# More Strassen pairs in groups 2 to 5, with the side work around them moved: a fused attention and SwiGLU kernel on one core

## The chip, the cores and the metric

The kernel runs on one core of a Trainium2 chip. The metric is the device time of one execution in microseconds; a kernel's time is the median of its timed runs. Below, PE is TensorE, DVE is VectorE, ACT is ScalarE, POOL is GpSimd and SP is SyncE. Each engine gets its instructions in one fixed order; the engines meet through semaphores.

The profile's own span (from first to last instruction) is some 1.8 us shorter than the device time of the same run.

Busy times hide short gaps. A matmul of 256 columns is recorded as 273 ns long, but in a full stream the next one starts after 109 ns; so a gap of up to some 0.16 us doesn't show in PE's busy time, and a wait in the list of waits is shown that much too short. Where it matters below, gaps are taken from the starts.

## The reference, cut to what matters

```python
def phi(x):
    return np.where(x > 0, x, np.exp(x) - 1.0) + 1.0
q_p, k_p = phi(q), phi(k)                          # q, k, v: (8, 8, 576, 64)
kv  = np.einsum('bhsd,bhse->bhde', k_p, v)
z   = np.sum(k_p, axis=2)
num = np.einsum('bhsd,bhde->bhse', q_p, kv)
den = np.einsum('bhsd,bhd->bhs', q_p, z)[..., None] + 1e-06
x   = (num / den) ...                              # reshaped to (4608, 512)
g   = x @ w_gate                                   # (512, 1536)
val = x @ w_val
out = (g * sigmoid(g) * val) @ w_out               # (1536, 512)
```

## The kernel before

The 4608 tokens are handled in nine groups of 512 (g = 0 to 8). For each group the attention output x is made ready; **layer 1** multiplies it with `w_gate` and `w_val` in twelve blocks of 128 columns and forms hT = silu(gate) * val; **layer 2** multiplies hT with `w_out`. The work for later groups (exp and max of k and q, the key-value product "J", the x product "M") is woven in between. In groups 2 to 8 layer 2 is done by Strassen's scheme, seven products in place of eight, and in layer 1 `NP[g]` *pairs* of blocks are done so too. In such a pair the gate and value products of two blocks are formed together, as seven products of four 256-column matmuls where the plain way has the columns of eight; the sums of weights that it needs are called W1 sums below (`wl_sum`), those of x `x_sum`, those of h `h_sums`.

```python
    hT = two([P, FB, U * C], FP16, "hT")           # two buffers, by group parity
    NP = {2: 0, 3: 2, 4: 2, 5: 2, 6: 6, 7: 6, 8: 6}
    # a plain block is four chunks of two 512-column matmuls
    def c_chunk(g, fb, k, pg, pv):
        (src, dst) = ((wg, pg), (wv, pv))[k // 2]
        def mm():
            for i in (2 * (k % 2), 2 * (k % 2) + 1):
                nc.tensor.matmul(out=dst[:, :], lhsT=src[:, i, P * fb:P * fb + P], rhs=xT[i][g % 2][:, :],
                                 start=(i == 0), stop=(i == 3))
        op("PE", 0.432, mm, ...)
        if k == 1:
            op("ACT", 0.52, lambda: silu_1(pg[:, :], s[:, :]), ...)
        if k == 3:
            op("DVE", 0.6, lambda: c_mul(g, fb, pv, s), ...)
    # a pair of blocks by Strassen: product n of 7, four 256-column matmuls each
    def pair_prd(g, p, n, bx, bz, by, h22):
        ...
        op("PE", 0.437, lambda: prd_1(g, p, n, dst), r, [nm(dst)])
        # n = 1, 5, 6: a copy on ACT; n = 2: silu; n = 7: a sum on DVE; n = 3: a sum on DVE, silu
        # n = 4: two products on DVE that write hT
    def casts(b):
        for lp in range(2):
            op("ACT", 1.07, lambda lp=lp: vcast(b, lp), ["v16"], [f"vm{lp}"])
    # end of layer 2 of group g: the loads of batch g + 3 are queued together
            for (f, x) in ((ld_k, "k16"), (ld_q, "q16"), (ld_v, "v16")):
                op("LD", 0.75, lambda f=f: f(b3), [], [x])
    XE = {g: "AVAA" for g in range(NG)}            # the four x copies: ACT, DVE, ACT, ACT
    WL = {2: [(m, c, 0) for m in range(4) for c in range(2)], 3: [...3...], 4: [...3...], 5: [...2...]}
    ORDER = {g: "10 11 20 21 60 61 50 51 70 71 30 M 31 40 J 41" for g in (2, 3, 4)}
    ORDER[5] = "10 11 20 21 60 61 50 51 70 71 M 30 31 | 40 41 J"
    ...
    for i in steps.split():                        # one fixed order of all operations
        ops[int(i)][2]()
```

Each `op` records an engine, an estimated duration, an action, and what it reads and writes. Nothing is emitted in the order in which it is recorded: the string `steps` lists all of them by number in one fixed order, and that order is what each engine gets. In `ORDER`, "40" is product 4 of token half 0, and so on.

Of the kernel before, what the change touches and what calls it, by code (L numbers as in the profile page):

```python
# [13 lines left out]
P = 128  # L14
# [3 lines left out]
def kernel(  # L18
# [54 lines left out]
    hT = two([P, FB, U * C], FP16, "hT")  # L73
# [5 lines left out]
    wl2 = sb.tile([P, 2, 10 * P], FP16, name="wl2")  # L79
# [216 lines left out]
    def l1_gate(g, fb):  # L296
        (pg, pv), s = l1_banks(g, fb), sil[fb % 2]
        nc.scalar.activation(out=s[:, :], in_=pg[:, :], func=AF.Silu, bias=0.0, scale=1.0)  # L298
        nc.vector.scalar_tensor_tensor(out=hT[g % 2][:, fb, :], in0=pv[:, :], scalar=SC, in1=s[:, :],  # L299
                                       op0=ALU.mult, op1=ALU.mult)  # L300
# [12 lines left out]
    def thirds(t):  # L313
        f = t.rearrange("p a b -> p (a b)") if len(t.shape) == 3 else t.rearrange("p a b c -> p (a b c)")
        return [f[:, 6 * P * i:6 * P * i + 6 * P] for i in range(3)]

    wl_all = [sum((thirds(t) for t in ts), []) for ts in (
        (k16[0][:, :, :], q16[0][:, :, :], v16[0][:, :, :]), (kp[0][:, :, :], wl2[:, :, :], vm[0][:, :, :, :]))]
# [50 lines left out]
    def c_mul(g, fb, pv, s):  # L369
        nc.vector.scalar_tensor_tensor(out=hT[g % 2][:, fb, :], in0=pv[:, :], scalar=SC, in1=s[:, :],  # L370
                                       op0=ALU.mult, op1=ALU.mult)
# [4 lines left out]
    def l2(g, t, f0=0, f1=FB):  # L376
        pso[(g, t)] = (pV[0], pG[0], pV[1], pG[1])[t]
        for fb in range(f0, f1):
            nc.tensor.matmul(out=pso[(g, t)][:, :], lhsT=hT[g % 2][:, fb, P * t:P * t + P], rhs=wo[:, fb, :],  # L379
                             start=(fb == 0), stop=(fb == FB - 1))  # L380
# [16 lines left out]
    def h_blk(g, kh, th, f0, f1):  # L397
        return hT[g % 2][:, 2 * f0 + kh:2 * f1 - 1 + kh:2, HT * th:HT * th + HT]
# [24 lines left out]
    def prd(g, n, tt, fs, seeded):  # L423
# [5 lines left out]
        def left(f):  # L429
            h = hT[g % 2]  # L430
# [273 lines left out]
    def k_block():  # L704
        for lp in range(2):
            exp_(k16, ek, 1, lp)
            plus_1(k16, kp, 1, lp)
        for lp in range(2):
            least(ek[:, 2 * lp:2 * lp + 2, :], kp, 1, lp)

    def q_block():
        nc.scalar.preload_act_table_set("natural_log_exp_and_others")
        es = [eq1[:, 2 * J * D * (1 - lp):2 * J * D * (2 - lp)].rearrange("p (l x) -> p l x", l=2) for lp in range(2)]
        for lp in range(2):
            nc.scalar.activation(out=es[lp], in_=q16[1][:, 2 * lp:2 * lp + 2, :], func=AF.Exp, bias=0.0, scale=1.0)
            plus_1(q16, qp, 1, lp)
        z0_copy(1, 0)
# [7 lines left out]

    def first():
        sl = at(FB, [(7, k_block)])
        w = at(17, [
            (3, lambda: num8()), (3, lambda: z0(1, 0)), (3, lambda: z0(1, 1)), (3, q_block), (3, lambda: x8()), (7, lambda: t1(0)), (8, lambda: t1(1)),
# [122 lines left out]
    def rh(g, fbs, ths=(0, 1)):  # L852
        return [f"h{g % 2}.{fb}.{th}" for fb in fbs for th in ths]
# [4 lines left out]
    NP = {2: 0, 3: 2, 4: 2, 5: 2, 6: 6, 7: 6, 8: 6}  # L858
# [16 lines left out]
    def pair_prd(g, p, n, bx, bz, by, h22):  # L875
# [22 lines left out]
        if n == 4:  # L898
            fbs = [2 * p, 2 * p + 1]
            op("DVE", 0.6, lambda: mul_1(bx, ALU.mult, sl0, hT[g % 2][:, 2 * p:2 * p + 2, 0:HN]),  # L900
# [3 lines left out]
               lambda: eng.tensor_tensor(out=hT[g % 2][:, 2 * p:2 * p + 2, HN:2 * HN], in0=v22, in1=sl1, op=ALU.mult),  # L904
# [29 lines left out]
    def casts(b):  # L934
        for lp in range(2):
            op("ACT", 1.07, lambda lp=lp: vcast(b, lp), ["v16"], [f"vm{lp}"])

# [24 lines left out]
    def x_prd(g, lps=(0, 1)):  # L962
# [9 lines left out]
        if NP[g] and 1 in lps:  # L972
            rs = ([rx(g, 0), rx(g, 1)], [rx(g, 2), rx(g, 3), "xs0"], [rx(g, i) for i in range(4)], [rx(g, 2), rx(g, 3), "xs1"])
            for m in range(4):
                op("DVE", 0.35, lambda m=m: x_sum(g, m), rs[m], [f"xs{m}"])

    XE = {g: "AVAA" for g in range(NG)}

    def l2_prd(g, n, tt, fs=tuple(range(HF))):
# [7 lines left out]
        if HF - 1 not in fs:  # L987
            return
# [51 lines left out]
    PARTS = {"": tuple(range(HF)), "a": (0, 1, 2, 3), "b": (4, 5), "c": (4,), "d": (5,), "e": (0, 1, 2, 3, 4)}  # L1040

    def layer_1(g, fill, head):
# [28 lines left out]
        else:  # L1071
            slots = {7 * p + 2 * i: (p, k) for p in range(6) for (i, k) in enumerate(PSEQ[p == 5])}
            for s in range(48):
# [5 lines left out]
                elif s > 40 and head:  # L1079
# [10 lines left out]
    PSEQ = ((1, 5, 6, 2, 7, 3, 4), (1, 5, 6, 3, 7, 2, 4))  # L1090
    ZB = {g: 2 for g in range(NG)}
    LEAD = {g: 3 for g in range(NG)}
    H22 = {g: ["DVE"] * 6 for g in range(NG)}
    SPLIT_2 = {g: ((0, 6),) if NP.get(g) != 6 else ((0, 3), (3, 6)) for g in range(NG)}
    SPLIT = {g: ((0, 3), (3, 5), (5, 6)) if NP.get(g) == 6 else ((0, 4), (4, 6)) for g in range(NG)}
    WL = {2: [(m, c, 0) for m in range(4) for c in range(2)], 3: [(0, 0, 1), (0, 1, 1), (1, 0, 1)], 4: [(1, 1, 1), (2, 0, 1), (2, 1, 1)], 5: [(3, 0, 1), (3, 1, 1)]}

    def layer_2(g, done):
# [3 lines left out]
        if b3 < B:  # L1102
            for (f, x) in ((ld_k, "k16"), (ld_q, "q16"), (ld_v, "v16")):
# [10 lines left out]
    def step(g, x):  # L1114
# [5 lines left out]
        else:  # L1120
            l2_prd(g, int(x[0]), int(x[1]), PARTS[x[2:]])
# [7 lines left out]

    def program():  # L1130
        op("DVE", 1.05, lambda: phi_q(3, 1), ["q16", "eq1"], rqp(3, lps=[1]))
        for (f, x) in ((ld_k, "k16"), (ld_q, "q16"), (ld_v, "v16")):
            op("LD", 0.75, lambda f=f: f(4), [], [x])
        tail = []
        for g in range(2, NG):
# [8 lines left out]
        0 1 14 15 17 4 16 35 2 36 8 19 18 38 3 5 39 37 41 40 20 42 6 44 45 43 47 21 46 48 50 49 51 22 53 52 25  # L1144
        54 23 56 57 55 59 24 58 60 26 62 63 61 65 64 27 66 9 68 67 69 71 28 70 72 74 73 29 75 112 77 76 115 78
        10 13 80 79 81 83 7 82 84 104 12 86 85 87 89 105 88 90 11 92 91 93 95 118 94 96 30 98 121 99 97 101 31
        100 102 110 127 103 129 32 128 106 131 120 107 133 108 130 135 114 132 134 137 109 139 138 136 116 141
        140 122 143 142 111 33 145 147 144 117 34 124 113 150 159 148 151 125 146 149 162 153 160 126 152 154
        161 165 163 119 123 164 172 155 168 180 170 167 171 173 181 157 166 183 174 169 156 201 182 175 202 184
        158 204 176 203 206 205 185 208 207 186 209 211 350 210 213 187 212 215 214 216 349 218 217 220 219 223  # L1150
        224 221 227 225 229 222 231 191 230 232 192 228 234 233 236 235 238 237 193 239 179 226 241 194 243 245
        240 244 246 242 249 188 178 247 251 254 189 255 248 257 252 256 190 195 258 250 260 261 259 263 262 253
        264 289 266 278 267 265 269 268 270 279 272 271 273 286 275 274 282 276 284 301 277 303 280 302 305 292
        304 285 281 307 306 283 309 288 311 308 287 313 310 298 312 290 315 294 196 317 295 314 319 316 197 291
        321 320 324 318 297 322 299 333 326 300 336 334 328 293 339 337 325 296 327 346 341 342 340 345 354 343
        344 331 347 355 198 357 329 356 375 199 376 358 359 378 377 330 380 200 323 379 335 338 382 348 381 332
        383 360 385 384 177 387 386 361 389 388 390 392 460 391 394 397 393 398 395 401 403 362 402 399 405 404
        406 363 352 408 410 463 364 412 409 411 413 365 407 415 466 414 417 469 419 416 418 420 396 366 423 353
        425 424 428 429 400 431 421 430 432 426 434 422 435 433 437 427 436 438 370 440 452 441 439 443 442 444
        453 446 445 447 449 367 448 456 450 458 475 451 477 454 476 479 523 478 459 481 455 480 483 457 462 485  # L1160
        482 461 487 484 472 486 489 464 488 465 491 368 493 490 492 369 468 467 495 498 494 496 507 473 500 502
        510 499 474 508 470 501 513 471 503 505 520 516 518 515 527 517 519 511 504 528 514 371 521 530 548 529
        549 506 531 372 551 532 550 524 553 552 555 554 556 533 558 373 557 560 559 562 534 374 561 563 497 509
        512 522 565 564 567 566 570 571 568 574 535 576 569 572 578 577 573 579 575 536 581 580 583 582 585 537
        584 586 633 588 636 587 639 590 589 538 592 525 591 593 596 539 598 526 601 597 602 599 604 603 605 594
        607 606 608 595 610 540 609 600 611 543 613 625 614 616 612 615 617 626 619 620 618 622 621 544 623 631
        645 624 647 627 646 649 628 648 629 638 651 653 650 632 652 655 640 657 654 630 656 659 635 634 661 545
        658 663 637 660 641 665 662 664 674 667 666 677 669 675 670 680 668 678 682 681 671 685 644 673 687 672
        541 690 688 683 546 692 542 686 691 642 699 547 676 679 697 696 684 695 693 689 701 694 700 698 703 643
        702 705 723 704 706 725 707 351 724 728 726 730 729 733 708 727 735 731 734 737 732 739 736 738 741 740  # L1170
        709 744 746 745 742 749 751 747 750 753 752 710 755 754 743 757 711 760 756 762 761 748 765 712 758 767
        766 769 763 768 771 770 759 773 776 772 774 778 777 764 781 775 779 783 782 785 811 787 784 780 789 786
        788 792 812 794 793 790 797 795 800 791 801 798 803 802 804 799 806 796 805 807 809 813 810 808 821 822
        823 824 825 815 814 828 830 832 829 834 816 836 819 831 843 826 833 835 838 845 818 844 847 820 846 817
        849 827 851 850 839 848 853 837 713 855 852 840 858 856 860 841 859 842 863 861 865 854 864 714 868 866
# [46 lines left out]
```

## Time and profile before

| | kernel before |
|---|---|
| device time, three runs at the start | 303.66 us (303.61 to 303.69) |
| span of the profiled run | 301.2 us |
| PE, DVE, ACT busy | 97%, 85%, 72% |
| start to group 2 | 85.14 us |
| groups 2, 3, 4, 5 | 31.59, 31.89, 31.07, 28.67 us |
| groups 6, 7, 8 | 29.43, 28.40, 30.25 us |

A group's length is counted from its first layer-1 matmul to that of the next group; for group 8 it ends with the last matmul. Since PE is nearly always busy, these lengths are the measure used in the whole text: what a group gains or loses is a gain or loss of the kernel.

The prediction below shows the page's head, the busy times group by group, the chain and the costliest groups. Three lines of PE's waits complete it (in total, times, longest, all in us):

```profile
PE pX L182 <- ACT osb L445: 0.5, 1, 0.5
...
PE pV L175 <- DMA v<-in_v_dram: 0.2, 1, 0.2
PE pG L866 <- ACT sil L364: 0.2, 1, 0.2
```

Waits of PE are few and short. The first stands at the key-value product J, which comes 3.3 us into group 6, the third in group 3 (the second is in the start-up). The table of transfers (KB each, then the median us from issue to landing) gives the loads that ACT waits for:

```profile
q<-in_q_dram POOLq DMA_DIRECT2D x7, 576.0 KB, 11.3
v<-in_v_dram POOLq DMA_DIRECT2D x7, 576.0 KB, 13.4
```

They have equal size, but v stands last in the queue of its batch and lands last.

### The profile page before, as it was taken

How to read it: one execution, taken by the hardware profiler on the slowest of the kernel's cores; microseconds unless marked ns; L12 is line 12 of the kernel's file. 1: busy time of each engine (PE TensorE's matmuls, PEld its weight loads, DVE VectorE, ACT ScalarE, POOL GpSimd, SP SyncE). 2: the span in 40 equal slices, each digit the busy share in tenths (PEclk: the TensorE clock that was granted, in tenths of full speed). 3: DMA queues.
4: the chain of work that ended last, by engine and by line, in shares of the span. 5: the costliest groups of instructions: out<-in, count | busy, mean ns of one | idle time of the engine just before them, and what ended most of it. 6: DMA issues, size and time to landing. Idle time of an engine off the chain costs nothing.

```text
span 301.2 us, 6998 instructions
## 1 busy us (share of the span) xinstructions
PE 292.4 (97%) x2764; PEld 197.2 (65%) x2764; DVE 256.8 (85%) x531; ACT 217.3 (72%) x361; POOL 42.3 (14%) x55
## 2 busy tenths in 40 slices
PE   7899999999999999999999999999999999999993
PEld 5644454444544486647665676668788888788882
DVE  4754658888899999979999999999999999948981
ACT  4873978948663699568868796879986689668841
POOL 8644346300010002000100020000000000000000
PEclk9999999999999999999999999999999999999998
DMA  7999999991699108930993089600730017023014
GB/s 209 193 196 201 206 208 213 204 168 26 112 187 159 27 2 136 253 67 4 163 203 65 0 142 177 140 0 3 143 76 2 3 26 167 0 64 79 2 36 105
DMA packets 41473, 32.89 MB, mean 109 GB/s; under 512 B 16400, under 2 KB 36816, under 8 KB 41440
## 3 DMA queue, kind: packets, MB, share of 16 engines
q0 software_dynamic: 20176, 18.35, 39.5%
q1 hardware_dynamic: 21104, 13.97, 20.9%
q8 instruction: 21, 0.34, 0.4%
q10 hardware_dynamic: 160, 0.13, 0.2%
q14 instruction: 12, 0.10, 0.1%
HBM read 37.75 MB, written 9.44 MB: 157 GB/s over the span
## 4 chain that ended last, share of the span: by engine, by line
PE 43%; issue 41%; DMA 7%; DVE 3%; ACT 3%; POOL 1%; POOLq 0%; ACTq 0%; DVEq 0%
DMA v<-in_v_dram 7%; PE pV L293 6%; PE pV L866 6%; PE pG L866 5%; PE pG L293 4%; PE pX L440 4%; PE pX L293 4%; PE pG L379 4%; PE pV L379 4%; PE pX L347 2%; PE pX L264 1%; PE pV L440 1%; ACT eq L125 1%; DVE hs L409 1%; DVE hT L370 1%
## 5 line engine op out<-in xcount | busy, mean ns | idle before, releaser
L866 PE MATMUL pV<-xt,wv 128*128 128x512 f16 x144 | 38.9, 379 | 0.0
L866 PE MATMUL pG<-xt,wg 128*128 128x512 f16 x144 | 38.4, 379 | 0.2 <-ACT sil L364 0.2
L364 ACT ACTIVATE sil<-pG 128x512 f16<-128x512 f32 x36 | 21.4, 597 | 20.0 <-PE pG L866 16.3
L440 PEld LDWEIGHTS <-hs 128*128 128x128 f16 x336 | 32.4, 98 | 5.1 <-issue 1.2
L440 PEld LDWEIGHTS <-hT 128*128 128x128 f16 x252 | 24.1, 98 | 5.0 <-DVE hT L370 0.4
L370 DVE SCALAR_TENSOR_TENSOR hT<-pV,sil 128x512 f16<-128x512 f32 x36 | 24.7, 686 | 2.0 <-ACT sil L364 1.3
L440 PE MATMUL pX<-ws,hs 128*128 128x256 f16 x210 | 25.2, 273 | 0.1
L866 PEld LDWEIGHTS <-wv 128*128 128x128 f16 x144 | 14.1, 98 | 12.6 <-issue 0.6
L866 PEld LDWEIGHTS <-wg 128*128 128x128 f16 x144 | 14.1, 98 | 12.4 <-issue 0.8
L299 DVE SCALAR_TENSOR_TENSOR hT<-pV,sil 128x512 f16<-128x512 f32 x21 | 14.2, 690 | 9.3 <-ACT sil L298 5.2
L293 PE MATMUL pV<-xt,wv 128*128 128x512 f16 x84 | 21.9, 379 | 0.0
L347 PEld LDWEIGHTS <-wg 128*128 128x128 f16 x192 | 18.7, 98 | 4.8
L100 POOL DMA_DIRECT2D k<-in_k_dram x7 | 5.2, 746 | 103.9 <-ACT part L449 51.8
L364 ACT ACTIVATE ek<-eq 128x512 f16<-128x512 f32 x24 | 15.0, 627 | 6.5 <-DVE eq L895 6.4
L449 ACT ACTIVATE part<-pX 128x256 f32<-128x256 f32 x35 | 12.5, 385 | 6.7 <-PE pX L440 6.6
L440 PE MATMUL pX<-wo,hT 128*128 128x256 f16 x126 | 17.1, 273 | 0.2 <-DVE hT L370 0.2
L1036 POOL DMA_DIRECT2D out_dram<-osb x1 | 0.6, 562 | 118.1 <-DVE osb L454 118.1
L232 DVE TENSOR_REDUCE den<-prod 128x12 f32<-128x768 f16 x18 | 17.0, 946 | 0.0
L347 PE MATMUL pV<-xt,wg 128*128 128x256 f16 x120 | 17.0, 273 | 0.0
L245 DVE TENSOR_TENSOR qp<-qp,rden 128x768 f16<-128x768 f16 x18 | 17.0, 949 | 0.0
L293 PEld LDWEIGHTS <-wv 128*128 128x128 f16 x96 | 9.4, 98 | 11.3
L125 ACT ACTIVATE ek<-k 128x1152 f16<-128x1152 f16 x14 | 15.8, 1159 | 1.3 <-DMA k<-in_k_dram 1.3
(201 smaller groups left out, 726.0 us busy)
## 6 DMA issues: line engine op xcount, KB each, us to landing
out_dram<-osb SPq DMA_DIRECT2D x64, 128.0 KB, 2.5
k<-in_k_dram POOLq DMA_DIRECT2D x7, 576.0 KB, 8.3
q<-in_q_dram POOLq DMA_DIRECT2D x7, 576.0 KB, 11.3
v<-in_v_dram POOLq DMA_DIRECT2D x7, 576.0 KB, 13.4
wg<-in_moe_w_gate_dram POOLq DMA_DIRECT2D x5, 256.0 KB, 9.5
wv<-in_moe_w_val_dram POOLq DMA_DIRECT2D x5, 256.0 KB, 10.0
wo<-in_moe_w_out_dram POOLq DMA_DIRECT2D x2, 512.0 KB, 15.1
out_dram<-osb SPq DMA_DIRECT2D x13, 64.0 KB, 2.0
```

Of the source, the lines that this page charges most:

```text
L125: nc.scalar.activation(out=e[:, s, :], in_=src[ix(b)][:, s, :], func=AF.Exp, bias=0.0, scale=1.0)
L232: nc.vector.tensor_reduce(out=den[:, HL * j0:HL * j1], in_=prod[:, 0:j1 - j0, :].rearrange("p j (l d) -> p (j l) d", d=D), axis=AX.X, op=A ...
L245: nc.vector.tensor_tensor(out=qv, in0=qv, in1=rden[:, HL * j0:HL * j1].unsqueeze(2).to_broadcast([P, HL * (j1 - j0), D]), op=ALU.mult)
L293: nc.tensor.matmul(out=ps[:, :], lhsT=src[:, i, P * fb:P * fb + P], rhs=xT[i][g % 2][:, :], start=(i == 0), stop=(i == 3))
L299: nc.vector.scalar_tensor_tensor(out=hT[g % 2][:, fb, :], in0=pv[:, :], scalar=SC, in1=s[:, :], op0=ALU.mult, op1=ALU.mult)
L347: nc.tensor.matmul(out=dst[:, HN * e:HN * e + HN], lhsT=lhs, rhs=rhs, start=(n in (1, 5) and e == 0 and c == 0), stop=(c == 1), skip_group ...
L364: nc.scalar.activation(out=dst, in_=src, func=AF.Silu, bias=0.0, scale=1.0)
L370: nc.vector.scalar_tensor_tensor(out=hT[g % 2][:, fb, :], in0=pv[:, :], scalar=SC, in1=s[:, :], op0=ALU.mult, op1=ALU.mult)
L379: nc.tensor.matmul(out=pso[(g, t)][:, :], lhsT=hT[g % 2][:, fb, P * t:P * t + P], rhs=wo[:, fb, :], start=(fb == 0), stop=(fb == FB - 1))
L440: nc.tensor.matmul(out=(z if n in (2, 3, 5) else x)[:, 0:HD], lhsT=left(f), rhs=right(f), start=(i == 0 and fs[0] == 0 and (n in (1, 5) or ...
L449: nc.scalar.activation(out=part[:, 2 * i + tt, :], in_=(x if from_x else z)[:, 0:HD], func=AF.Copy, bias=0.0, scale=1.0 / SC)
L866: nc.tensor.matmul(out=dst[:, :], lhsT=src[:, i, P * fb:P * fb + P], rhs=xT[i][g % 2][:, :], start=(i == 0), stop=(i == 3))
```

## The change

Its intent: let three pairs of every group from 2 to 5 run by Strassen, which takes matmul columns off the full PE, and make room for their cost on DVE and ACT. For this the W1 sums go to group 0, where DVE has idle; the memory for them comes from hT, which loses its second buffer; one x copy goes from DVE to ACT; v is loaded a group earlier; and the products at the hand-over from one group to the next are reordered. The core of the diff (renamings of hT, and the string `steps`, which is new as a whole, are cut):

```diff
-    hT = two([P, FB, U * C], FP16, "hT")
+    hT = sb.tile([P, FB, U * C], FP16, name="hT")
-    wl2 = sb.tile([P, 2, 10 * P], FP16, name="wl2")
+    wl_0 = sb.tile([P, 8, 6 * P], FP16, name="wl_0")
+    wl_1 = sb.tile([P, 3, 6 * P], FP16, name="wl_1")
...
     def first():
-        sl = at(FB, [(7, k_block)])
+        sl = at(FB, [(4, lambda: wl_pair(0, 0)), (5, lambda: wl_pair(1, 0)), (6, lambda: wl_pair(2, 0)), (7, k_block),
+                     (7, lambda: wl_sum(3, 1, 0))])
...        # four more W1 sums in group 0's other blocks
-    NP = {2: 0, 3: 2, 4: 2, 5: 2, 6: 6, 7: 6, 8: 6}
+    NP = {2: 3, 3: 3, 4: 3, 5: 3, 6: 6, 7: 6, 8: 6}
...
     def casts(b):
         for lp in range(2):
             op("ACT", 1.07, lambda lp=lp: vcast(b, lp), ["v16"], [f"vm{lp}"])
+        if b + 1 < B:
+            op("LD", 0.75, lambda: ld_v(b + 1), [], ["v16"])
...
-    XE = {g: "AVAA" for g in range(NG)}
+    XE = {g: 'AAAA' for g in range(NG)}
...
-    LEAD = {g: 3 for g in range(NG)}
+    LEAD = {g: 1 for g in range(NG)}
-    SPLIT = {... ((0, 4), (4, 6)) ...}
-    WL = {2: [(m, c, 0) for m in range(4) for c in range(2)], 3: [...3...], 4: [...3...], 5: [...2...]}
+    SPLIT = {... ((0, 2), (2, 4), (4, 6)) ...}
+    WL = {2: [(1, 1, 1), (2, 0, 1)], 3: [(2, 1, 1)], 4: [(3, 0, 1)], 5: [(3, 1, 1)]}
...
-            for (f, x) in ((ld_k, "k16"), (ld_q, "q16"), (ld_v, "v16")):
+            for (f, x) in ((ld_k, "k16"), (ld_q, "q16")):
...
+    ORDER.update({g: "10 11 20 21 60 61 50 51 70 71 30 31 M 41 J 40" for g in (2, 3, 4)})
+    ORDER[5] = "10 11 20 21 60 61 50 51 70 71 M 30 31 | 41 40 J"
```

## The prediction

> **What bounds the kernel now.** I read four views of the kernel before, in this order: the head of the page, the busy time of each engine group by group, the chain that ended last, and the groups of instructions with their shapes kept apart. The head of the page:
>
> ```profile
> span 301.2 us, 6998 instructions
> PE 292.4 (97%) x2764; PEld 197.2 (65%) x2764; DVE 256.8 (85%) x531; ACT 217.3 (72%) x361; POOL 42.3 (14%) x55
> ...
> PE   7899999999999999999999999999999999999993
> ...
> DVE  4754658888899999979999999999999999948981
> ```
>
> PE is busy 97% of the span, and its row of digits has 9s everywhere but in the first two slices and the last. So the kernel is bound by matmul work and by the few holes in it, and a change gains by removing matmul columns or holes. But the DVE row also shows 9s from the end of group 1 to group 7: the mean of 85% hides a stretch where a second engine is almost full. The busy times of groups 2 to 5 (from the first layer-1 matmul of one group to that of the next; columns: stretch, its length, then busy us and instruction counts of each engine) show how full:
>
> ```profile
> core 0: us, PE busy (x) PEld busy (x) DVE busy (x) ACT busy (x) POOL busy (x), PEclk, DMA share, GB/s
> 85.14:116.72 31.58, 31.58 (x270) 18.54 (x269) 30.51 (x59) 21.31 (x34) 3.70 (x5) 1.00 0.57 87
> 116.72:148.62 31.90, 31.54 (x296) 20.82 (x293) 29.99 (x63) 24.36 (x42) 2.22 (x3) 1.00 0.68 126
> 148.62:179.69 31.07, 30.95 (x295) 20.95 (x293) 30.25 (x65) 23.55 (x40) 2.22 (x3) 1.00 0.60 106
> 179.69:208.36 28.67, 28.67 (x211) 19.10 (x209) 27.93 (x59) 22.61 (x41) 0.00 (x0) 1.00 0.47 91
> ```
>
> The four lengths sum to 123.2 us, DVE's busy times to 118.7 us (96%), ACT's to 91.8 us. DVE has 4.5 us of idle in the very groups that are to get more Strassen pairs. Also: groups 3 and 4 do the same matmul work, and group 3 takes 0.83 us longer. The order of time inside group 3 shows why:
>
> ```profile
> 129.68 1.19 ACT L156 ACTIVATE vm<-v 128x1152 f16<-128x1152 f16 x1 [2.39 <-DMA v<-in_v_dram]
> ...
> 133.91 0.69 DVE L370 SCALAR_TENSOR_TENSOR hT<-pV,sil 128x512 f16<-128x512 f32 x1 [1.26 <-ACT sil L364]
> 133.93 1.02 PE L866 MATMUL pG<-xt,wg 128*128 128x512 f16 x4 [0.17 <-ACT sil L364]
> ```
>
> ACT, which is in order, stands 2.39 us at the cast of v whose load has not landed; the silus behind it are late, DVE loses 1.26 us and PE some too. The chain that ended last passes through this load:
>
> ```profile
> 105.37 0.86 PE pV L866 x4
> 106.24 1.97 PE pX L440 x18
> ...
> 115.79 13.86 DMA v<-in_v_dram
> ```
>
> Its last line is that load, 13.86 us from issue to landing. The first two give the spacing of matmuls in an unbroken stream: 0.86/4 = 0.216 us at 512 columns, 1.97/18 = 0.109 us at 256.
>
> **What the Trainium skill says.** "TensorE: Matmul & The Clock Gate", section "Back-to-back issue gap": N/2.4 + 2.5 ns warm, 518 cycles for 512 columns and 262 for 256, that is 216 and 109 ns. The trace agrees to the ns. (The same section's sustained 131 ns for N=512 is not what this trace has.) So two 256-column matmuls cost 1% more than one of 512 and Strassen keeps nearly its whole saving in columns. "Perfetto Trace Analysis", section "DVE / Act Engine Instruction": the recorded window runs to the write's acknowledgement, while the next instruction may start reading earlier; so durations of neighbours overlap. The trace agrees: the 686 ns products in the table below follow each other every 0.60 us. I therefore charge DVE by start-to-start spacing in full stretches. "DMA: Bandwidth & Descriptors", section "Rules for kernel authors": issue the DMA early and wait on it late; the v load above is the counterexample.
>
> **The change part by part.** First the rows that carry the costs (busy us, mean ns of one, idle before):
>
> ```profile
> L370 DVE SCALAR_TENSOR_TENSOR hT<-pV,sil 128x512 f16<-128x512 f32 x36 | 24.7, 686 | 2.0 <-ACT sil L364 1.3 <-PE pV L866 0.3
> ...
> L895 DVE TENSOR_TENSOR eq<-pX,rr 128x512 f32<-128x512 f32 x15 | 10.2, 682 | 0.3 <-PE pX L347 0.2
> ...
> L904 DVE TENSOR_TENSOR hT<-r,ek 128x512 f16<-128x512 f16 x24 | 9.7, 414 | 0.0
> ...
> L336 DVE TENSOR_TENSOR xs<-xt 128x512 f16<-128x512 f16 x12 | 4.9, 415 | 0.1
> ...
> L328 DVE TENSOR_TENSOR kp<-wv 128x768 f16<-128x768 f16 x2 | 1.1, 557 | 0.0
> ```
>
> 1. *Pairs.* A pair is two of the twelve 128-column blocks of layer 1. Plain, it is 16 matmuls of 512 columns, 16 x 0.216 = 3.46 us; Strassen, 7 products of 4 matmuls of 256 columns, 28 x 0.109 = 3.06 us. Saved: 0.40 us. The pairs of groups 2, 3, 4, 5 go from 0, 2, 2, 2 to 3 each: six more. **PE: -2.4 us**, all on the path, since PE is full there.
>
> 2. *What the pairs cost elsewhere.* On DVE a plain pair is two fused products, 2 x 0.60 = 1.20 us in spacing; a Strassen pair is three such 512-wide PSUM operations (the third is the L895 kind) and one SBUF product at 0.33: 2.15 us. So +0.95 a pair, +5.7 us for six. Group 2 also gets its four input sums, 4 x 0.33 = 1.3 us. On ACT a pair goes from 2 to 5 passes of about 0.5 us in spacing: +1.5 each.
>
> 3. *W1 sums.* All 16 lie in groups 2 to 5 now. The new order puts 11 into group 0 and leaves 5: at 0.47 us spacing **-5.2 us of DVE in groups 2-5**. In group 0's layer 1 DVE is busy 10.1 of 19.9 us, so I count them free there.
>
> 4. *x copies.* The second of the four copies moves from DVE (0.60) to ACT in the hand-overs out of groups 2 to 5: -2.4 us of DVE, +2 us of ACT. The sums of h are cut into three pieces in place of two: about 0.15 us more DVE a group, +0.6.
>
> DVE in groups 2-5: +5.7 +1.3 -5.2 -2.4 +0.6 = 0.0. **The same 118.7 us of DVE work now has to fit into a shorter stretch.** ACT: 91.8 + 6 x 1.5 + 2 = 103 us, which fits.
>
> 5. *v a group ahead.* The load is queued after the previous casts, some 25 us ahead of use in place of 14. Group 3's excess of 0.83 us over group 4 should go, and with it a part of the late start of group 4. **About -1.0 us.**
>
> 6. *One hT buffer.* Layer 1's first write of hT comes after a matmul chunk that stands behind the last products of layer 2 in PE's own order, so I expect no new wait; what it gives is room for the W1 sums. *Hand-over order:* the key-value product J now comes ahead of product 40 and x copies get product 41, J and 40 (about 2.0 us) to run beside: no gain in columns, perhaps 0.3 us of small holes.
>
> Sum if nothing new waits: -2.4 - 1.0 - 0.3 = -3.7 us, giving 300.0. The PE time of groups 2-5 would be 123.2 - 3.7 = 119.5 us against 118.7 of DVE, which leaves 0.8 us of idle in 119.5 where DVE had 4.5. An in-order engine that also waits for PE and ACT will hardly be 99% busy. Part is helped: the order shows the group 2 input sums and two of its W1 sums ahead of group 2's first product, some 2.2 us that group 1 can take (DVE's digits are 8 there). I choose 0.9 us of new PE waits from a late DVE. **Predicted: 303.7 - 3.7 + 0.9 = 300.9 us.**
>
> **The rivals.** (a) *DVE becomes the bound of groups 2-5.* For it: 96% now, same work, shorter stretch; layer 2 starts only two chunks after the last pair, where it had fifteen plain chunks of slack in groups 3-5. Against it: the two pairs of group 4 ran with no visible PE wait. If DVE cannot rise above the 96% it has, groups 2-5 need 118.7/0.963 = 123.2 us, the whole gain is lost and the time is about 303.5. (b) *Nothing new waits:* 300.0, or 299.5 if the holes at the start of group 6 close too (a 0.5 us wait for ACT before its key-value product shows in the waits). (c) *The v load was hidden anyway,* as PE waits only 0.17 us directly: then only pairs count, about 301.9 with the same 0.9 of waits. Against it: group 3's 0.83 us. (d) *The W1 sums delay group 0,* whose layer 2 goes through DVE for the transposed q and the second batch: three of the sums stand there. At most 3 x 0.47 = 1.4 us, giving 302.3; there DVE is busy 11.1 of 15.3 us, so I give it little.
>
> **Range and chances.** 299.5 is all of (b), 302.8 is half of the gain lost to (a) or (d) together; between them I expect the time 8 times in 10. 2% is 6.1 us, well beyond the 3.7 us that the parts can give, so faster by over 2% gets 3%. Slower by over 2% would need the new waits to reach 10 us: 2%.
>
> **What would show it.** Right: the Strassen groups of layer 1 count 168 more matmuls of 256 columns and the plain ones 96 fewer of 512; groups 2-5 together last 119.5 to 120.5 us with DVE at 98% or more; the idle of ACT before the vm cast is gone; groups 3 and 4 last equally long. Wrong: PE waits for hT, hs or xs sums at the start of layer 2 or inside pairs summing to over 2 us (a); group 0 longer than in the kernel before (d); a vm cast that still waits for its load.

## The result, and the profile after

| | before | after |
|---|---|---|
| device time, median (four runs each, same rounds) | 303.63 us (303.13 to 303.69) | **299.00 us** (298.75 to 299.29) |
| ratio after / before | | 0.9851, 95% interval 0.9834 to 0.9868 |
| span of the profiled run | 301.2 us | 297.2 us |
| start to group 2 | 85.14 | 85.39 |
| group 2, 3, 4, 5 | 31.59, 31.89, 31.07, 28.67 | 30.40, 30.54, 30.40, 28.27 |
| group 6, 7, 8 | 29.43, 28.40, 30.25 | 28.94, 28.40, 30.12 |

A ratio is the mean time of one kernel's runs over that of the other's of the same rounds, so it is not quite the ratio of the medians. 299.0 lies 0.5 us under the low end of the range. The kernel gained more than I had allowed for. A second comparison of the same two kernels gave 299.18 against 303.19 us, so the gain is 4.0 to 4.6 us by the medians; the difference comes from the runs of the kernel before, whose medians were 303.19 to 303.63 us over six comparisons.

The head of the page after, to be set against that in the prediction:

```profile
span 297.2 us, 7177 instructions
PE 289.4 (97%) x2836; PEld 204.5 (69%) x2836; DVE 260.6 (88%) x549; ACT 228.1 (77%) x385; POOL 42.9 (14%) x55
...
PE   7899999999999999999999999999999999999993
...
DVE  4767889888899999999999999999999989948981
```

PE has 72 matmuls more, which are 168 more of 256 columns and 96 fewer of 512, and is busy 3.0 us less. DVE's digits have become larger at the front (4, 7, 6, 7 for 4, 7, 5, 4), where the W1 sums now are. The busy times of groups 2 to 5, in the columns of the prediction's table:

```profile
85.39:115.79 30.40, 30.40 (x306) 22.06 (x305) 29.66 (x60) 25.91 (x45) 2.72 (x4) 1.00 0.49 85
115.79:146.33 30.54, 30.54 (x307) 22.02 (x305) 30.12 (x65) 25.92 (x46) 2.48 (x4) 1.00 0.75 129
146.33:176.73 30.40, 30.40 (x308) 22.10 (x305) 30.02 (x68) 26.01 (x46) 1.48 (x2) 1.00 0.59 106
176.73:205.00 28.27, 28.27 (x223) 20.36 (x221) 27.91 (x59) 23.65 (x43) 0.74 (x1) 1.00 0.47 88
```

In each row the second number, PE's busy time, equals the first, the length. The same four groups as one stretch, first before, then after:

```profile
85.14:208.36 123.22, 122.74 (x1065) 79.41 (x1064) 118.68 (x241) 91.83 (x155) 8.14 (x11) 1.00 0.58 103
```

```profile
85.39:205.00 119.61, 119.61 (x1137) 86.54 (x1136) 117.71 (x248) 101.49 (x176) 7.41 (x10) 1.00 0.58 103
```

The stretch became 3.61 us shorter; DVE is busy 117.71 of 119.61 us, 98.4%, up from 96.3%, and yet PE shows no idle in it. One gap is too short for this view: in group 3 a product that reads a sum of x from DVE starts 0.13 us late (at 118.31 us), which is why group 3 is 0.14 us longer than groups 2 and 4. The list of PE's waits shows none of groups 2 to 8 either. These lines are from its top, and all of them lie in the start-up or in group 0:

```profile
PE pX L493 <- DVE sil L482: 1.3, 1, 1.3
...
PE pX L265 <- ACT rr L559: 0.3, 1, 0.3
```

The waits for a silu in group 3 and for `osb` at group 6 are gone. Lastly the casts of v in group 3, which stood 2.39 us before, and the transfers:

```profile
119.65 1.17 ACT L157 ACTIVATE vm<-v 128x1152 f16<-128x1152 f16 x1
121.67 1.20 ACT L157 ACTIVATE vm<-v 128x1152 f16<-128x1152 f16 x1
```

```profile
q<-in_q_dram POOLq DMA_DIRECT2D x7, 576.0 KB, 7.9
v<-in_v_dram POOLq DMA_DIRECT2D x7, 576.0 KB, 7.8
```

Neither cast has an idle time in brackets after it. The casts also come earlier now: 119.65 is 3.9 us into group 3, where before it was 13.0 us. And v no longer queues behind k and q: it lands in 7.8 us instead of 13.4.

The gain by groups is 1.19 (g2), 1.35 (g3), 0.67 (g4), 0.40 (g5), 0.49 (g6), 0 (g7) and 0.13 us (g8), 4.23 in all; the front gives back 0.25. Which part of the change each of these belongs to was the question for the experiments.

### The profile page after: what moved, and what is told of

It is laid out like the page before. It is cut to its first block, busy times and chain, and to the rows that moved or that the text cites. A ratio compares the mean times of both kernels' runs of the same rounds, so it can differ in the third digit from the quotient of the medians.

```text
span 297.2 us, 7177 instructions
## 1 busy us (share of the span) xinstructions
PE 289.4 (97%) x2836; PEld 204.5 (69%) x2836; DVE 260.6 (88%) x549; ACT 228.1 (77%) x385; POOL 42.9 (14%) x55
## 4 chain that ended last, share of the span: by engine, by line
PE 55%; issue 38%; DMA 2%; ACT 2%; POOL 0%; POOLq 0%; ACTq 0%
PE pX L348 8%; PE pX L441 7%; PE pV L294 6%; PE pG L874 5%; PE pV L874 5%; PE pG L294 4%; PE pX L294 4%; PE pG L380 4%; PE pV L380 4%; DMA q<-in_q_dram 2%; PE pV L441 2%; PE pV L348 1%; PE pX L265 1%; PE pX L183 1%; PE pV L265 0%
## 5 line engine op out<-in xcount | busy, mean ns | idle before, releaser
L348 PEld LDWEIGHTS <-wl 128*128 128x128 f16 x390 | 38.1, 98 | 15.1 <-DVE xs L337 0.7
L348 PEld LDWEIGHTS <-wg 128*128 128x128 f16 x240 | 23.4, 98 | 7.9
L874 PE MATMUL pG<-xt,wg 128*128 128x512 f16 x96 | 28.5, 379 | 0.0
L874 PE MATMUL pV<-xt,wv 128*128 128x512 f16 x96 | 27.9, 379 | 0.0
L348 PE MATMUL pX<-xs,wl 128*128 128x256 f16 x180 | 27.0, 273 | 0.0
L294 PE MATMUL pV<-xt,wv 128*128 128x512 f16 x84 | 21.9, 379 | 0.0
L362 ACT ACTIVATE rr<-pX 128x512 f32<-128x512 f32 x33 | 19.5, 597 | 2.9 <-PE pX L348 2.6
L300 DVE SCALAR_TENSOR_TENSOR hT<-pV,sil 128x512 f16<-128x512 f32 x21 | 14.2, 690 | 6.6 <-ACT sil L299 4.4
L365 ACT ACTIVATE ek<-pV 128x512 f16<-128x512 f32 x30 | 17.8, 595 | 2.6 <-PE pV L348 2.3
L365 ACT ACTIVATE sil<-pG 128x512 f16<-128x512 f32 x24 | 14.3, 594 | 5.4 <-PE pG L874 5.4
L294 PEld LDWEIGHTS <-wv 128*128 128x128 f16 x96 | 9.4, 98 | 11.3
L371 DVE SCALAR_TENSOR_TENSOR hT<-pV,sil 128x512 f16<-128x512 f32 x24 | 16.5, 686 | 0.6 <-PE pV L874 0.2
```

The source lines that it names most:

```text
L294: nc.tensor.matmul(out=ps[:, :], lhsT=src[:, i, P * fb:P * fb + P], rhs=xT[i][g % 2][:, :], start=(i == 0), stop=(i == 3))
L300: nc.vector.scalar_tensor_tensor(out=hT[:, fb, :], in0=pv[:, :], scalar=SC, in1=s[:, :], op0=ALU.mult, op1=ALU.mult)
L348: nc.tensor.matmul(out=dst[:, HN * e:HN * e + HN], lhsT=lhs, rhs=rhs, start=(n in (1, 5) and e == 0 and c == 0), stop=(c == 1), skip_group ...
L362: nc.scalar.activation(out=dst, in_=halves(src), func=AF.Copy, bias=0.0, scale=scale)
L365: nc.scalar.activation(out=dst, in_=src, func=AF.Silu, bias=0.0, scale=1.0)
L371: nc.vector.scalar_tensor_tensor(out=hT[:, fb, :], in0=pv[:, :], scalar=SC, in1=s[:, :], op0=ALU.mult, op1=ALU.mult)
```

## The experiments

Sixteen kernels were run, all correct. "Before" in each comparison is a set of runs of the kernel before on the same chip. Lengths are of groups 2, 3, 4, 5, then 6, 7, 8 where they differ from those of the kernel that was edited. To move an operation, only its place in the string `steps` changes.

| label | edit | us | before | ratio |
|---|---|---|---|---|
| after_again | none | 299.18 | 303.19 | 0.9865 |
| before_early_v | kernel before, v loads early | 301.68 | 303.19 | 0.9953 |
| late_v | after, v loads late | 325.98 | 303.19 | 1.075 |
| old_handover_5 | after, old order out of group 5 | 299.12 | 303.19 | 0.9862 |
| x_copy_dve | after, one x copy back on DVE | 299.95 | 303.31 | 0.9883 |
| dve_plus4, 8, 16 | after, extra DVE sums | 299.68, 300.40, 303.43 | 303.31 | 0.9874, 0.9900, 1.0000 |
| w1_sums_late | after, 11 W1 sums behind group 1 | 304.77 | 303.50 | 1.0043 |
| before_one_hT | kernel before, one hT | 303.68 | 303.50 | 1.0012 |
| before_table_late, before_no_holes | kernel before, ACT order at group 6 | 304.30, 302.64 | 303.50 | 1.0026, 0.9974 |
| before_table_late2, before_no_holes2 | the same, another order | 303.34, 301.85 | 303.25 | 1.0002, 0.9950 |
| before_no_holes3 | one more move | 301.84 | 303.19 | 0.9950 |
| table_early | after, the table load early | 299.09 | 303.25 | 0.9858 |

### Is the result real?

The changed kernel once more, with more rounds.

> The changed kernel once more, as the measure for the runs beside it: 299.0 us, span about 297.2 us, no wait of PE in groups 2 to 5. Theory A (the gain is 2.4 us of matmul columns plus some 1.7 us of holes in groups 3, 4 and 6) and theory B (part of the gain of 4.6 us is chance in the runs of the kernel before) both expect this; B would let the ratio to the kernel before move by 0.2% or more.

Measured: 299.18 us (298.87 to 299.51), ratio 0.9865 (0.9848 to 0.9882), all seven lengths as in the first profile. The gain stands, at 4.0 us here.

### The v load

Theory A: the late v load caused the excess of group 3 and part of group 4. Rival: the load was hidden, and the gain of group 3 came from the new order as a whole. First, the kernel before with nothing changed but the place of its four v loads. Each goes right behind the casts that free its buffer:

```diff
 # places in the order of operations
-  v(4) behind operation 38; v(5) behind 160; v(6) behind 326; v(7) behind 499
+  v(4) first of all; v(5) behind the casts of v(4); v(6) behind those of v(5); v(7) behind those of v(6)
```

> The kernel before with nothing changed but the place of three loads of v (and the first v ahead of k and q): each is queued right after the casts that free its buffer. Theory A: the 2.39 us wait of the vm cast goes and with it the holes of groups 3 and 4, so the time falls by 1.0 to 1.4 us to about 302.4, groups 3 and 4 last the same 30.8 us. Rival (the load was hidden, since PE itself waits 0.17 us): 303.6, no change. If it falls by more than 1.4 us, the timed runs of the kernel before wait longer for v than its profiled run did (profiled run 302.96, timed 303.6).

Measured: 301.68 us, ratio 0.9953 (0.9937 to 0.9969). Group 3 went from 31.89 to 30.79, group 4 from 31.07 to 30.98, the others did not move: 1.19 us. In the change, groups 3 and 4 gained 2.02 us, of which 0.80 is one pair each (0.40, see below). The remaining 1.22 us is close to what the load alone is worth. Theory A holds, and in sum its size is right too. By groups it is less even: beyond its pair group 3 gained 0.95 us in the change against 1.10 here (the change has the late product named above), and group 4 gained 0.27 against 0.09 (a product that sums z, early in the group, starts 0.28 us late in the kernel before, 0.19 here, and on time in the change).

Then the opposite: the changed kernel with its v loads back behind the q load of their batch.

```diff
 # places in the order of operations
-  v(4), v(5), v(6), v(7): right behind the casts of the batch before
+  v(4), v(5), v(6), v(7): right behind the q load of the same batch
```

> The changed kernel with each v load back behind the q load of its batch, all else as changed. Theory A: the hole in group 3 comes back, since the vm casts stand now even earlier in the group: +1.0 to +2.0 us, about 300.0 to 301.0, and ACT waits over 2 us for v. Rival (hidden): 299.0.

Measured: 325.98 us (ratio 1.075), lengths 30.40, 38.06, 35.11, 41.83. The direction was right, the size wrong by far. Of PE's waits, in us in total, times, longest; and ACT's first cast of group 3:

```profile
PE pX L348 <- ACT pV L362: 19.3, 3, 11.4
```

```profile
125.38 1.18 ACT L157 ACTIVATE vm<-v 128x1152 f16<-128x1152 f16 x1 [5.30 <-DMA v<-in_v_dram]
```

Because v is there early, the new order puts the casts near the start of a group. With v late, ACT stands at the cast, and everything behind it in ACT's stream, first of all the copies of the Strassen products, is late; one wait took 11.4 us. PE waited 19.3 us, and the three groups grew by 25.8. Nearly all of the rest is clock: the granted clock reads 0.50 from 127.96 to 134.79 us, from 165.51 to 168.92 and from 203.06 to 213.29, and after each of the three waits like instructions of PE start 0.85 us apart where 0.43 is usual, which costs some 6 us in all. So the early load is not an optional part of this version: the order is built on it.

### The order of products out of group 5

My theory for the 0.49 us at group 6 was the swap of products 40 and 41. The changed kernel with the old order there:

```diff
-    ORDER[5] = "10 11 20 21 60 61 50 51 70 71 M 30 31 | 41 40 J"
+    ORDER[5] = "10 11 20 21 60 61 50 51 70 71 M 30 31 | 40 41 J"
```

> The changed kernel with only the hand-over from group 5 to 6 in its old order: product 40, then 41, then J, in place of 41, 40, J. J of batch 7 writes bank X1, which product 41 fills and ACT must empty first. Theory A: PE waits again about 0.5 us before J, group 6 lasts 29.4 us in place of 28.9, time +0.5 us to 299.5. Rival (the hole came from a late ACT and would be gone with the new schedule anyway): 299.0.

Measured: 299.12 us, every length as in the changed kernel, 28.94 at group 6. The theory fell: the swap does not change the length. By the starts it only moves a little idle: with the old order the gap before J is 0.20 us in place of 0.09, and one later in the group 0.06 in place of 0.16. The swaps out of groups 2 to 4 were not tried by themselves.

### How full may DVE be?

The prediction had charged 0.9 us because DVE would be about 99% busy. It was 98.4% busy by its records, and PE lost 0.13 us. Two rivals: DVE still has room (an addition is free), or DVE is just below its limit (each added us costs one). First, the second x copy back on DVE:

```diff
-    XE = {g: 'AAAA' for g in range(NG)}
+    XE = {g: 'AVAA' for g in range(NG)}
```

> The changed kernel with the second x copy of each hand-over back on DVE (0.60 us each, in the hand-overs to groups 3 to 8). DVE was busy 117.7 of 119.6 us in groups 2 to 5 without one wait of PE. Theory of the prediction (an in-order DVE near full makes PE wait): 2.4 us more DVE work than the 1.9 us of idle, so PE waits 1 to 2.5 us in groups 2 to 6 and the time is 300 to 301.5. Theory A (DVE can be filled to the last few tenths before PE notices, its lag is taken up by work that nobody waits for soon): +0.5 us or less.

Measured: 299.95 us, lengths 30.40, 30.84, 30.59, 28.33, then 29.20, 28.48, 30.12: together 0.89 us more, for six copies of 0.60 us moved onto DVE (3.6 us). The copy is the only work of the hand-over that changed, so in the full version this part is worth 0.9 us. In groups 3 and 6 some 0.26 us each of it stands right at the start, where an early matmul of layer 1 that reads x is that much late: so the copy seems to count by its place in the hand-over, and not only as load on DVE.

Then a dose: extra sums with 768 columns on DVE, written into a tile that nobody reads any more (0.47 us each by the spacing of the W1 sums), spread evenly over groups 2 to 5.

```diff
+    seen = 0
     for i in steps.split():
         ops[int(i)][2]()
+        if ops[int(i)][0] == "DVE" and seen < 224:
+            seen += 1
+            if seen % 56 == 28:                     # % 28 == 14 for 8 sums, % 14 == 7 for 16
+                nc.vector.tensor_tensor(out=flat(kp[0])[:, 0:6 * P], in0=wg[:, 0, 0:6 * P], in1=wg[:, 1, 0:6 * P], op=ALU.add)
```

> The changed kernel with 4 idle DVE sums of 768 columns (0.47 us each, 1.9 us in all) spread over groups 2 to 5, into a dead tile. It fills the 1.9 us of DVE idle. Prediction's theory: +0.9 us or more. Theory A: 0 to +0.5 us.

> The same with 8 sums, 3.8 us: 1.9 us beyond the idle. Both theories expect about +1.9 us at least; prediction's theory +2.8. If it stays under +1, work can spill into groups 1 and 6 to 8, and DVE is not a bound even now.

> The same with 16 sums, 7.5 us: 5.6 us beyond the idle. The time should rise by about 5.6 us to 304.6 if DVE then bounds groups 2 to 5 one for one.

| extra sums | extra work (x 0.47) | groups 2-5 | more than without | DVE busy |
|---|---|---|---|---|
| 0 | 0 | 119.61 us | 0 | 98.4% |
| 4 | 1.9 us | 120.24 | 0.63 | 98.8% |
| 8 | 3.8 us | 120.95 | 1.34 | 99.3% |
| 16 | 7.5 us | 123.86 | 4.25 | 99.6% |

Device times were 299.68, 300.40 and 303.43 us. The first 1.9 us cost 0.33 us per us, the next 1.9 cost 0.38, the last 3.8 cost 0.77. In these arrangements neither rival is right: there is no free room at 98.4%, but the price is a third at first and rises toward one. Place and amount were not separated, though. The cost is local (with 4 sums three products start late, by 0.27, 0.26 and 0.12 us, which is all of the 0.63), and each dose was tried in one arrangement; the same sums at other places might cost more or less. Two lines of PE's waits with 16 sums, which the changed kernel does not have:

```profile
PE pX L348 <- DVE r L368: 1.0, 3, 0.4
PE pX L348 <- DVE xs L337: 0.8, 1, 0.8
```

PE now waits for DVE to free the bank of a pair and for the sums of x, which is rival (a) of the prediction, in a kernel made for it. With 7.5 us of work added to DVE, the whole gain is gone: the ratio is 1.0000.

### The W1 sums

The changed kernel with its 11 sums of group 0 behind group 1, ahead of group 2's work:

```diff
-        wl_sum(3, 0, 0) ...                         # all 11 in group 0
+    for (m, half) in ((0, 0), (1, 0), (2, 0), (3, 0), (0, 1)):
+        wl_pair(m, half)
+    wl_sum(1, 0, 1)
     program()
```

> The changed kernel with its 11 early W1 sums taken out of group 0 and put on DVE in one row at the end of group 1, 11 x 0.47 = 5.2 us of DVE just ahead of group 2's first pair. Theory (DVE's order is what matters; the first pair of group 2 needs 8 of them): PE waits 2.5 to 5 us around the start of group 2, time 301.5 to 304, and groups 0 and 1 get no faster than in the changed kernel. Rival (DVE's slack in group 1, 4.2 us, takes them): 299.5 or less.

Measured: 304.77 us, ratio 1.0043, over the 304 expected at most. The stretch before group 2 took 85.40 us against 85.39 with the sums in group 0, but the start-up in it varies by more than the sums could cost. Layer 2 of group 0, where three of them stand, repeats better. Before, then after, in the columns of the prediction's table:

```profile
36.45:51.73 15.28, 15.28 (x216) 7.39 (x216) 11.14 (x27) 12.14 (x16) 7.52 (x6) 1.00 1.22 208
```

```profile
36.42:51.98 15.56, 15.53 (x215) 7.48 (x214) 13.78 (x30) 12.13 (x16) 8.15 (x6) 1.00 1.22 208
```

It took 15.3 us in every profile of a kernel without sums there, this one included, and 15.5 to 15.6 us in all nine with them. So in group 0 the sums are nearly free: they cost 0.2 to 0.3 us, which is the prediction's rival (d) at a fifth of its 1.4 us. Group 2 became 35.74 us long, 5.34 more, for 11 x 0.47 = 5.2 us of sums. PE at the wait (start, us, instruction, idle before it):

```profile
90.81 1.01 PE L348 MATMUL pX<-xs,wl 128*128 128x256 f16 x4 [3.73 <-DVE xs L337]
91.62 1.06 PE L871 MATMUL pV<-xt,wv 128*128 128x512 f16 x2
...
94.00 0.60 PE L348 MATMUL pV<-xt,wg 128*128 128x256 f16 x4
94.44 0.59 PE L871 MATMUL pG<-xt,wg 128*128 128x512 f16 x2
```

The wait itself is 3.73 us. After it, the starts of like instructions lie about 0.85 us apart until 94.0, and 0.43 us afterwards: PE ran at half its rate for about 3.2 us (the granted clock reads 0.50 from 90.39 to 93.81 us) and lost some 1.6 us beyond the wait. A single long hole thus cost about 1.4 times its length. It was the place of the sums, not their number, that cost.

### One hT buffer

The kernel before with one hT buffer and nothing else:

```diff
-    hT = two([P, FB, U * C], FP16, "hT")
+    hT = sb.tile([P, FB, U * C], FP16, name="hT")
```

> The kernel before with a single hT buffer and nothing else. Prediction's step 6 (no new wait, since layer 1's first write follows a matmul that stands behind layer 2's last read): all group lengths the same to 0.05 us, time the same as the kernel before. Rival: a write of hT waits for layer 2 in some group, 0.3 us or more a group.

Measured: 303.68 us, ratio 1.0012, all lengths as before. The second buffer bought no time; giving it up is free.

### The hole at the start of group 6

After the order of products had fallen as a cause, ACT's stream there was looked at. In the kernel before (start, us, instruction, idle before it):

```profile
209.94 1.28 ACT L947 ACT_TABLE_LOAD   x1
211.23 0.66 ACT L445 ACTIVATE osb<-pX 128x256 f32<-128x256 f32 x2
211.78 0.60 ACT L361 ACTIVATE rr<-pX 128x512 f32<-128x512 f32 x1
```

and PE behind it:

```profile
211.66 0.22 PE L182 MATMUL pX<-vm,kp 64*64 64x65 f16 x2 [0.52 <-ACT osb L445]
```

The key-value product J needs a bank (`pX`, where matmuls leave results) that the copies to `osb`, the finished output rows of layer 2, set free, and they stand behind the load of the silu table, 1.28 us. In the changed kernel these copies stand ahead of it (the table load starts at 208.44, the copies at 206.33 and 207.38). The theory: the place of the table load is the hole. In the kernel before the load was moved, with and without early v:

```diff
 # places in the order of operations, ACT at the start of group 6
-  table load, osb, osb, copy, copy
+  osb, osb, table load, copy, copy               # before_table_late, before_no_holes
+  osb, copy, osb, copy, table load               # before_table_late2, before_no_holes2
+  the last, and the copies of R behind zd        # before_no_holes3
```

> The kernel before with one ACT instruction moved: the 1.28 us table load at the start of group 6 now stands behind the two osb copies that followed it. The old hand-over order in the changed kernel had not brought the 0.68 us hole of PE before J back, so theory A' says the hole came from this table load, which held up the copy that empties bank X1. Expected: PE's wait for osb is gone, group 6 lasts 28.8 to 29.0 us in place of 29.43, time 0.5 us lower (302.7 if the kernel before gives 303.2). Rival (the hole comes from J's bank order or from ACT being behind in general): group 6 still 29.4.

> The kernel before with both moves: v loads early and the table load late; no pair, no W1 sum, no copy moved. If gains add: -1.2 - 0.5 = -1.7 us, groups 2 to 6 of 31.6, 30.8, 30.8 to 31.0, 28.7, 28.9 us, time about 301.5 where before gives 303.2. What then remains to the changed kernel (2.4 us in the group lengths) is the six pairs.

Measured: 304.30 and 302.64 us; group 6 got longer, 30.33 and 30.32 us against 29.43. By the starts, the idle before J shrank from 0.69 to 0.20 us, where an undisturbed one is 0.09. But now a product of layer 1 waits for the copy behind the table load:

```profile
PE pG L347 <- ACT rr L361: 0.9, 1, 0.9
```

So the hole had moved, and grown. The second order, with the load behind all four:

> The kernel before with four copies on ACT (two osb copies and two copies of layer 1 of group 6) in the changed kernel's order and the table load behind all four. Theory (the table load's place on ACT makes the hole of group 6): group 6 lasts 28.9 us in place of 29.43, time 0.5 us less than the kernel before. Rival (ACT is behind in the kernel before for other reasons): 29.3 us or more.

> The kernel before with that and the early v loads: groups 2 to 6 of 31.6, 30.8, 31.0, 28.7, 28.9 us, 1.7 us less than the kernel before in the trace, some 301.6 where before gives 303.3. The changed kernel is then 2.4 to 2.6 us ahead in group lengths, the six pairs at 0.40 us.

Measured: 303.34 and 301.85 us, group 6 at 29.73 us. Now the product that sums z waited 0.84 us, since the copies of R (J's result, brought to fp16) stand behind the table load. These put behind the work on z too:

> The kernel before with early v loads, the table load of group 6 behind four copies, and in addition the two R copies of batch 7 behind the four zd products that read the same banks. Theory (two orders on ACT made group 6's hole: table load ahead of the copies that empty banks, R copies ahead of zd): group 6 lasts 28.9 to 29.0 us in place of 29.43, group 3 30.8, and the time is 0.55% (1.7 us) under the kernel before. Rival (something else holds group 6): 29.4 or more.

Measured: 301.84 us (ratio 0.9950, 0.9934 to 0.9966), group 6 at 29.48 us, again not shorter than 29.43: the idle before J is 0.20 us and two holes of 0.27 and 0.31 us come later. Last, the test the other way: the changed kernel with its table load ahead of the same four copies.

> The changed kernel with only the table load of group 6 moved ahead of the same four copies, as in the kernel before. Theory: the hole of PE comes back, group 6 lasts 29.4 to 30.0 us in place of 28.94, time +0.5 to +1.0 us. Rival: 28.94.

Measured: 299.09 us; group 6 at 29.23 us, 0.29 longer, and the wait is back:

```profile
PE pX L183 <- ACT osb L446: 0.4, 1, 0.4
```

So the place of the table load does make the hole in front of J, from both sides, but for its last 0.1 us, which goes with the old order of products 40 and 41. But in the kernel before no single move gained the half microsecond: it wandered along ACT's in-order stream. Which parts of the new order keep it closed behind J as well stays open; so does the 0.13 us of group 8, which no run looked at. The traces show where it is: in the kernel before a product of layer 2 that reads hT starts 0.15 us late, 22.6 us into the group, and in the changed kernel none does there.

No version was found that beats the changed kernel. No run changed the number of pairs alone: their worth is read from the group lengths.

## Why the prediction was wrong

It gave 300.9 us, 299.5 to 302.8; measured were 299.0 us. Point by point:

1. **Pairs: right.** Group 5, where no hole was involved, went from 28.67 to 28.27 us, 0.40 for one pair; group 2, with three, gained 1.19. Six pairs are the 2.4 us of the prediction.
2. **DVE's balance: nearly right.** "The same 118.7 us of DVE work": 117.71 us were measured. ACT has 101.5 us, predicted 103.
3. **W1 sums free in group 0: nearly.** DVE's busy time there rose from 21.2 to 27.9 us over the two parts of group 0, and its layer 2 grew by 0.3 us (15.28 to 15.56), which the run with the sums elsewhere does not show. Group 2 starts 0.25 us later in the profile after; the start-up varies by more than that.
4. **v load: right cause, a little too small.** I said 1.0 us, the load alone is worth 1.2 us in the kernel before. Rival (c), a hidden load, is refuted.
5. **One hT buffer: right**, no wait, by a run of its own.
6. **Hand-over order: not where I saw it.** The 0.3 us allowed for small holes became 0.6 (0.49 at group 6, 0.13 at group 8), and the swap of products out of group 5 has no part in it. With one x copy back on DVE, group 6 lost 0.26 us.
7. **The step that failed: "I choose 0.9 us of new PE waits from a late DVE."** Measured: 0.13 us, the one late product of group 3. I had set 118.7 us of DVE work against 119.5 us of time and argued that "An in-order engine that also waits for PE and ACT will hardly be 99% busy". The yardstick was wrong. The 118.7 us are busy time by recorded durations, and a record outlasts the start of the next instruction, as the prediction itself says (a product on DVE is recorded as 686 ns long, the next starts after 0.60 us), so that short idles vanish in it. Here is an estimate from the traces: each DVE instruction of groups 2 to 5 is charged with the usual distance from its start to the next, by shape, over six profiles (0.60 us for 512 columns from PSUM, 0.33 for a sum of 512 in SBUF). In the changed kernel this gives about 112 us of work, 94% of 119.6. By this estimate DVE had some 7 us of room and not 0.8; even with 16 sums more it comes to about 96%. Whether it also helped that much of DVE's work has no PE instruction close behind it (the sums and products for batches ahead), and may slip, I did not show.

Without that term the same sum gives 300.0 us, the prediction's rival (b), and with the holes as measured: 303.7 - 2.4 - 1.2 - 0.6 = 299.5 us, or 299.7 with the 0.25 us that the front gives back, which lies in the range. The rest is the starting point: the first three runs of the kernel before, 303.66 us, were at the upper end of its later medians (303.19 to 303.63), and against the run by the side of the trace the gain is 4.0 us (span 301.2 to 297.2). So the missing 0.9 us is a fault of the prediction, but that the time fell just under the range is in part the luck of these runs. The rival "half of the gain lost to (a)" set the upper end and was far off; the low end was placed exactly at the best case that I had written down, with no allowance for a hole being larger than it looked. That is the second mistake: the holes were sized from single lines (0.83 us between two groups, part of a 0.5 us wait), and both allowances turned out too small. The 0.5 us wait was 0.69 us by the starts.

Of the signs named in advance: 168 more small and 96 fewer large matmuls, yes; groups 2 to 5 at 119.5 to 120.5 us with DVE at 98% or more, yes (119.61, 98.4%); no idle before the casts, yes; groups 3 and 4 alike, but for the 0.14 us of the late product (30.54 and 30.40). They held, and none of them decided the 0.9 us. The sign for (a) would have, PE waits of over 2 us, and there were none. The sign for (d), a longer group 0, came true by 0.3 us in its layer 2.

## What to carry to other kernels

When one engine is full, write down the length of each stage between fixed instructions of it: here such lengths repeat to 0.02 us, except where a load is waited for, while the total wanders by 1 us, and effects of 0.3 us can be told apart. A second engine that is recorded as 96% busy is not yet a bound: add up the distances from start to start in place of the durations, find out who waits for its work and when, and move what nobody waits for to a stage with idle, as the W1 sums here. A load that is made early lets an order be built that depends on it; then it cannot be undone by itself. And a hole in an in-order stream may only wander when one instruction is moved, as at group 6 here.

## What the Trainium skill lacked or had wrong

- "TensorE: Matmul & The Clock Gate", section "Back-to-back issue gap", gives 131 ns per matmul as the sustained spacing for 512 columns and calls N/2.4 + 2.5 ns an isolated gap that is too long there. In the unbroken streams of these runs, each matmul with its own weight load, the spacing is 0.86/4 = 0.216 us at 512 columns, which is the formula's, and 0.109 us at 256. No run shows 131 ns. Other sections of the page have the formula as the measured back-to-back spacing, which is what is seen here.
- The same page, section "What's actually happening", has about 3.4 us of idle as what throttles PE's clock to half and 3.4 us of work as what restores it. The run with late W1 sums agrees: in a wait of 3.73 us the granted clock fell to 0.50, and it stayed there for 3.42 us. In the run with late v a wait of 3.15 us by the starts was enough (the clock fell at 165.51 us), a little less than the page has.
- "ScalarE: Activation LUTs", section "What ACT_TABLE_LOAD costs", gives 1283 ns for the load plus a drain of about 1380 ns. The load is 1.28 us here, but the next ACT instruction starts 1.29 us after the load's start (209.94 to 211.23), and the load itself starts 0.02 us after the recorded end of the instruction before it, so a drain shows neither behind it nor ahead of it.
- No page that I found says how busy a second in-order engine may be before the first waits. Here 98.4% by recorded durations (some 94% by the distances from start to start, an estimate) brought one wait of 0.13 us. In the arrangements tried, added work cost 0.33 us per us up to 98.8%, and 0.77 between 99.3% and 99.6%.
